# Chunk 1's x^T from 64x32 tiles, with its denominators inverted between two VectorE turns

## The chip, the cores and the metric

The kernel runs on one core of a Trainium2 chip. The metric is device time in microseconds (us) for one execution; three runs of the kernel before gave 258.91, 259.48 and 259.96, median 259.48. The engines are named as in the profile: PE (TensorE, matmuls), PEld (its weight loads), DVE (VectorE), ACT (ScalarE), POOL (GpSimd), SP (SyncE, which here only issues DMAs).

## The reference

An attention with sketched features, and behind it an MLP with an exact GELU:

```python
# q, k, v: (4 batches, 4 heads, 1088 tokens, 32); S1, S2: (8, 32)
def phi(x):
    a = np.einsum('rd,bhsd->bhsr', S1, x)
    b = np.einsum('rd,bhsd->bhsr', S2, x)
    return np.einsum('bhsi,bhsj->bhsij', a, b).reshape(*x.shape[:-1], r * r)
q_p, k_p = (phi(q), phi(k))
kv = np.einsum('bhsf,bhsd->bhfd', k_p, v)
z = np.sum(k_p, axis=2)
num = np.einsum('bhsf,bhfd->bhsd', q_p, kv)
den = np.einsum('bhsf,bhf->bhs', q_p, z)[..., None] + 1e-06
attn_out = (num / den).astype(np.float32)
# x: (4352 tokens, 128 = 4 heads * 32)
h = x @ w_in                                  # w_in: (128, 2048)
g = 0.5 * h * (1.0 + erf(h / np.sqrt(2)))
out = (g @ w_out).astype(np.float32)          # w_out: (2048, 128)
```

w_in, w_out, S1 and S2 arrive as 64-bit floats. The kernel rounds them to 32 bits itself, from the two words of each number.

## The kernel before

The 4352 tokens are eight chunks of 512 (two for each batch) and a last one of 256. x^T of a chunk is a tile of 128 features by 512 tokens. A hidden slice `hidden(n, fi)` (L715) is one matmul of 128 columns of w_in with x^T of chunk n into one of two PSUM banks h_ps, and a GELU on ACT out of it. An output product `project(n, fi)` (L847) adds a slice times its part of w_out to chunk n's o_ps. Chunks 0 and 1 do their first eight slices in this way (`steps`, L964), and everything behind them with seven products in place of eight. The matmul of the first slice stands apart as `first_hidden` (L730): in quarters for chunk 0, in halves for chunk 1.

The order on every engine is the order of the text: each instruction is tied to the one before it on its engine (L1219), so an instruction that waits holds up all behind it on its engine.

Batch 0's keys and values are reduced first into kz[0] (L930), which has 64 features for two pairs of heads on its partitions, and for each head 32 columns of kv and one of z. Then chunk 0 and chunk 1 get their x^T. `expand_products(n)` (L533) multiplies the turned queries with both sketches on PE, ACT copies one factor (`expand_copy`, L548), and DVE multiplies the two into q_pT (`expand_multiply`, L552). In the kernel before, both chunks go on alike: `numerators_by_token` (L648) makes, in tiles of 64x64 with 33 columns, numerators and denominators with tokens on the partitions; `divide` (L663) divides on DVE; `turn_half` (L698) or `turn_half_apart` (L690) transposes the quotient on PE, and ACT or DVE copies it out of PSUM into xT. For chunk 1 this stands in the loop over the steps at t = 3 (L1175 to L1187), with chunk 0's output products among it. Later chunks take another way (`query_outer`, `attend`, L584 to L644) with 64x32 tiles at L633; for batch 0's part of the last chunk they read `kz_first`, which `repeat_first_z` (L498) fills by two ACT copies.

Rounding of a weight piece (class `Rounding`, L243): `low_words` (ACT, L260), two `fields` (DVE, L268 exponent and L273 mantissa), `exponents` (ACT, L279), `mantissas` (DVE, L287, or ACT L284 and POOL L285), `signs` (DVE, L292) and `product` (L297, DVE or POOL). The first two pieces of w_in and of w_out hold 256 columns each. w_in[0]'s product is on POOL; behind it POOL writes one word into the landing place of w_out[0] and of w_out[1] (L180), and SP's queue, which issues in order, has these two transfers waiting for that (L181), and all later weights, keys, values and queries behind them.

In the opening, lines L923 to L961 set the order: chunk 0's numerators and division, chunk 1's expansion, rounding of w_in[1] between the divisions, chunk 0's first slice, chunk 1's q_pT.

Of the kernel before, what the change touches and what calls it, by code (L numbers as in the profile page):

```python
# [8 lines left out]
FP = mybir.dt.float32  # L9
U32 = mybir.dt.uint32  # L10
AX = mybir.AluOpType
# [5 lines left out]
def kernel(  # L17
# [28 lines left out]
    REM = S - MAIN  # L46
    JC = 4
    CW = JC * 128
    G = 128 // 32
    NCH = J // JC  # L50
    C = D + 1
# [25 lines left out]
    def hidden_bank():  # L77
        return hps.tile([128, CW], FP, name="h_ps")

    def out_bank():  # L80
        return ops.tile([128, CW], FP, name="o_ps")

# [144 lines left out]

    kz = [big.tile([128, 128], FP, name=f"kz{b}") for b in range(B)]

    kz_first = big.tile([128, 128], FP, name="kz_first")  # L230

    ones = big.tile([128, D], FP, name="ones")

# [255 lines left out]
    def sketch_of_z(b, ps, at):  # L489
# [5 lines left out]
        dve.tensor_mul(out=S_abc[b][:, :, :, 4:8], in0=c.rearrange("p (i f) -> p i f", i=2)[:, :, None].broadcast_to([128, 2, 2, 4]),  # L495
                       in1=own_r[:, None, :, None].broadcast_to([128, 2, 2, 4]))

    def repeat_first_z():  # L498

        of = kz[0].rearrange("f (r x) -> f r x", r=2)  # L500
        to = kz_first.rearrange("f (c r d) -> f c r d", c=NP, r=2)
        for c in range(NP):
            act.copy(out=to[:F, c], in_=of[c * F:(c + 1) * F, :, 0:D])
        zs = att.tile([128, 2, D], FP, name="z_cols")
        pool.tensor_copy(out=zs, in_=of[:, :, D:C].broadcast_to([128, 2, D]))
        held["zs"] = zs
# [26 lines left out]
    def expand_products(n):  # L533


        W = width[n]
        for i in range(2):
            B_of[n, i] = work_banks()
        for s in range(2):
            for g in range(G):  # L540
                for c in range(NP):
                    rows = slice(g * D, (g + 1) * D)
                    pe.matmul(B_of[n, g // 2][c * F:(c + 1) * F, g % 2, s * W // 2:(s + 1) * W // 2],  # L543
                              lhsT=Srep[rows, s].rearrange("p i j -> p (i j)"),
                              rhs=qT[n][rows, 2 * c:2 * c + 2].rearrange("p r j t -> p r (j t)"), start=True, stop=True)
        qp[n] = att.tile([128, 2, CW], FP, name="q_pT")

    def expand_copy(n, i):  # L548
# [2 lines left out]

    def expand_multiply(n, i):  # L552
        W = width[n]
        a, b = (t.rearrange("f g (r x) -> f g r x", r=2) for t in (A[i][:, :, :W // 2], B_of[n, i][:, :, W // 2:W]))
        dve.tensor_mul(out=qp[n].rearrange("f r (g x) -> f g r x", g=G)[:, 2 * i:2 * i + 2], in0=a, in1=b)

# [64 lines left out]
    def attend_products(n, banks=None):  # L621


        W = width[n]
        m = 1 if n < NMAIN else B // 2
        banks = work_banks() if banks is None else banks
        f = qp[n].rearrange("f r x -> f (r x)")[:, :2 * W].rearrange("f (c i n r t) -> f c i n r t", c=NP, i=m, r=2, t=32)
        N = W // 2 // m
        for i in range(m):
            for s in range(2):  # L630
                rows, b = slice(s * 64, (s + 1) * 64), batch_of(n, s, i)
                for h in range(H):
                    pe.matmul(banks[h * D:(h + 1) * D, s, i * N:(i + 1) * N],  # L633
                              lhsT=(kz[b] if b else kz_first)[rows, h * D:(h + 1) * D],
                              rhs=f[rows, h // 2, i, :, h % 2], start=True, stop=True)
        numerators_in[n] = banks

    def take_x(n):

        W, banks, m = width[n], numerators_in.pop(n), 1 if n < NMAIN else B // 2  # L640
        xT[n] = att.tile([128, CW], FP, name="xT", bufs=3)
        to = xT[n][:, :W]
        to = to.rearrange("p (s x) -> p s x", s=2) if m == 1 else to.rearrange("p (s t i) -> p s i t", s=2, i=m)
        act.copy(out=to, in_=banks[:, :, :W // 2] if m == 1 else banks[:, :, :W // 2].rearrange("p s (i t) -> p s i t", i=m))  # L644

    x_tok = {}

# [92 lines left out]

    blocks, sums, acc = {}, {}, {}
    T = {}
    HW = CW // 2
    NPAIR = NF // 2

    PLACE = {"1": (0, 0, 0), "2": (0, 0, HW), "3": (1, 0, 0), "5": (1, 0, HW),
# [175 lines left out]
    kv_first_rem(kv_bank)  # L922
    w_in = [Rounding(w) for w in w_in_sb[:2]]  # L923
    w_in[0].low_words()
    w_in[0].fields()
    w_in[0].exponents()
    late = []
    query_turn(1, lambda **a: late.append(a))
# [7 lines left out]
    w_out = [Rounding(w, beside=b) for w, b in zip(w_out_sb[:2], w_in)]  # L936
    by_act(**late[0])
    w_in[1].low_words()
    parts = [range(2), range(2, JC)]
    nd = [[hidden_bank(), hidden_bank()], [out_bank(), out_bank()]]  # L940
    for banks, tokens in zip(nd, parts):
        numerators_by_token(0, banks, tokens)
    den = denominators(nd[1])
    expand_products(1)
    divide(0, nd[0], parts[0], by_head_pair=True)
    w_in[1].exponent_fields()
    w_in[1].exponents()
    divide(0, nd[1], parts[1], by_head_pair=True, den=den)
    turn_half(0, 0, hidden_bank(), by_act)
    w_in[1].mantissa_fields()  # L950
    turn_half_apart(0, 1, [out_bank(), out_bank()])
    w_in[1].mantissas()
    w_in[1].signs()
    w_in[1].product()
    for half in range(2):
        first_hidden(0, half)
    for i in range(2):
        expand_copy(1, i)
    for i in range(2):
        expand_multiply(1, i)  # L960
    w_out[0].fields()  # L961


    steps = [(n, fi) for f in range(0, USUAL, 4) for n in range(NCH) for fi in range(f, f + 4)]  # L964
# [199 lines left out]
    for t in range(len(steps) + LAG):  # L1164
        if t < 4:

            hidden(0, t)
            if t == 1:
                w_out[0].low_words()
                w_out[0].exponents()  # L1170
                w_out[0].finish()
                w_out[1].fields()
            if t == 2:
                w_out[1].low_words()
            if t == 3:  # L1175
                banks = work_banks()
                numerators_by_token(1, halves(banks), range(JC))
                w_out[1].mantissas(by_pool=True)
                w_out[1].exponents()
                divide(1, banks, range(JC), by_head_pair=False)  # L1180
                w_out[1].signs()
                w_out[1].product()
                project(0, 0)
                project(0, 1, cols=slice(0, 256))
                turn_half(1, 0, work_bank(), by_act)
                project(0, 1, cols=slice(256, 512))
                turn_half(1, 1, work_bank(), by_dve)  # L1187
            continue
        if t == 4:
            first_hidden(1, 0)  # L1190
            for f, *a in products[t]:
                f(*a)
            first_hidden(1, 1)
        for n in drains[t]:
            drain(n)
        sooner = t == NMAIN * NF
        if sooner:
            for f, *a in products[t]:
                f(*a)
        if t < len(steps):  # L1200
            n, fi = steps[t]
            hidden(n, fi, by_halves=t >= 18 and (n < NMAIN or fi < 5))
        if t < len(steps) and steps[t][0] < NMAIN and steps[t][1] % NB == NB - 1:
            n, b = steps[t][0], steps[t][1] // NB
            if b >= first_block(n):
                token_sums(n, b)
        for f in slots[t]:
            f()
        for n in done[t]:
            store(n)  # L1210
        if t != 4 and not sooner:
            for f, *a in products[t]:
                f(*a)
    for n in done[len(steps) + LAG]:
# [40 lines left out]
```

## Time and profile before

| what | value |
|---|---|
| time, median of three runs | 259.48 us |
| span of the profiled execution, first to last instruction | 258.0 us |
| time of the profiled execution itself | not given apart; the three runs are 258.91 to 259.96 us |
| granted TensorE clock | 1.000 |
| DVE, ACT, POOL busy | 151.0, 115.5, 163.5 us |
| chunk 1's x^T, from its numerators' start to its last turn's end on PE | 19.11 to about 22.4 us |
| chunk 1's first hidden slice, starts of its two halves | 22.45 and 23.81 us |

The profile is that of one execution. A row of a timeline has a start and a length in us from the first instruction, the engine, the line, the operation, the tile written and the tiles read, and the count of instructions that were merged into the row; in brackets stands idle time and what ended it. A 32-bit matmul is recorded as two instructions, a transpose as one. Matmuls are pipelined, so the start of the next row tells more than the length of one.

### The profile page before, as it was taken

The numbers are of one execution on the slowest core, as the hardware profiler recorded it, in microseconds if no ns is written. First come the engines' busy times: TensorE is split into PE (matmuls) and PEld (weight loads), VectorE is DVE, ScalarE is ACT, GpSimd is POOL, SyncE is SP. The second block draws the span as 40 slices with busy tenths as digits, with TensorE's granted clock in tenths as the row PEclk, the third lists the DMA queues.
The fourth block names the chain that finished last, engine by engine and source line by source line (L and its number), as shares of the span: only waits on it lengthen the run. The fifth ranks groups of instructions, "written<-read, shape, count | busy, mean of one in ns | idle before, by whom it ended". The sixth has DMA issues, their size and how long they took to land.

```text
span 258.0 us, 5769 instructions
## 1 busy us (share of the span) xinstructions
PE 253.9 (98%) x2335; PEld 136.1 (53%) x2335; DVE 151.0 (59%) x312; ACT 115.5 (45%) x224; POOL 163.5 (63%) x173
## 2 busy tenths in 40 slices
PE   8999999999999999999999999999999999999995
PEld 7856444345444545544444455455444444445794
DVE  2786888969699997590187986399307000700330
ACT  4685777443626332443335332533444334433442
POOL 3403006799968788487758775787758777877300
PEclk9999999999999999999999999999999999999999
DMA  6469848721000101102000002000200200020020
GB/s 199 144 185 374 188 95 217 213 76 14 3 0 12 31 1 21 23 6 37 3 0 3 0 9 38 0 1 3 41 3 4 39 0 1 7 36 0 3 41 20
DMA packets 29594, 13.48 MB, mean 52 GB/s; under 512 B 21888, under 2 KB 27776, under 8 KB 29568
## 3 DMA queue, kind: packets, MB, share of 16 engines
q1 hardware_dynamic: 29392, 13.05, 20.3%
q8 instruction: 18, 0.29, 0.5%
q10 hardware_dynamic: 176, 0.07, 0.1%
q14 instruction: 8, 0.07, 0.1%
HBM read 10.88 MB, written 2.23 MB: 51 GB/s over the span
## 4 chain that ended last, share of the span: by engine, by line
PE 98%; DVE 1%; issue 0%; ACT 0%; DVEq 0%
PE h_ps L721 45%; PE o_ps L807 33%; PE o_ps L858 5%; PE w_ps L855 3%; PE w_ps L437 1%; PE w_ps L890 1%; PE w_ps L578 1%; PE w_ps L633 1%; PE o_ps L426 1%; PE h_ps L737 1%; PE w_ps L978 1%; PE w_ps L656 0%; PE w_ps L543 0%; DVE x_tok L679 0%; PE h_ps L333 0%; PE w_ps L333 0%
## 5 line engine op out<-in xcount | busy, mean ns | idle before, releaser
L721 PE MATMUL h_ps<-xT,w_in 128*64 128x512 f32 (+3 forms) x514 | 136.9, 576 | 0.0
L728 ACT ACTIVATE block<-h_ps 128x512 f32<-128x512 f32 (+1 forms) x128 | 73.0, 571 | 117.3 <-PE h_ps L721 115.3
L721 PEld LDWEIGHTS h_ps<-xT,w_in 128*64 128x64 f32 (+1 forms) x514 | 41.9, 143 | 30.4 <-issue 11.6
L807 PE MATMUL o_ps<-block,w_out 128*64 128x256 f32 x224 | 57.5, 379 | 0.0
L772 POOL TENSOR_TENSOR bits_low<-block 128x512 f32<-128x512 f32 x28 | 35.9, 1281 | 27.8 <-ACT block L728 27.8
L807 PEld LDWEIGHTS o_ps<-block,w_out 128*64 128x64 f32 x224 | 30.5, 137 | 38.0 <-issue 27.5
L773 POOL TENSOR_TENSOR bits_a<-block 128x512 f32<-128x512 f32 x28 | 35.7, 1277 | 12.0 <-ACT block L728 11.9
L822 DVE COPY sums<-o_ps 64x256 f32<-64x256 f32 x8 | 3.3, 416 | 60.6 <-PE o_ps L807 60.6
L774 POOL TENSOR_TENSOR bits_e<-bits_a,block 128x512 f32<-128x512 f32 x28 | 36.0, 1286 | 2.2
L775 POOL TENSOR_TENSOR bits_m<-block,bits_e 128x512 f32<-128x512 f32 x28 | 35.8, 1279 | 2.2
L807 PE MATMUL o_ps<-bits_low,small 128*64 128x256 f32 x112 | 28.8, 380 | 0.0
L807 PE MATMUL o_ps<-bits_a,small 128*64 128x256 f32 x112 | 28.8, 380 | 0.0
L807 PE MATMUL o_ps<-block,small 128*64 128x256 f32 x112 | 28.8, 379 | 0.0
L807 PE MATMUL o_ps<-bits_m,w_out 128*64 128x256 f32 x112 | 28.8, 380 | 0.0
L807 PEld LDWEIGHTS o_ps<-block,small 128*64 128x64 f32 x112 | 15.2, 137 | 17.9 <-issue 10.8
L807 PE MATMUL o_ps<-bits_e,small 128*64 128x256 f32 x112 | 17.1, 383 | 0.0
L858 PE MATMUL o_ps<-g,w_out 128*128 128x512 f32 (+1 forms) x34 | 16.5, 572 | 0.0
L807 PEld LDWEIGHTS o_ps<-bits_m,w_out 128*64 128x64 f32 x112 | 15.4, 137 | 0.0
L807 PEld LDWEIGHTS o_ps<-bits_a,small 128*64 128x64 f32 x112 | 15.2, 137 | 0.0
L807 PEld LDWEIGHTS o_ps<-bits_low,small 128*64 128x64 f32 x112 | 15.2, 137 | 0.0
L590 DVE STREAM_TRANSPOSE w_ps<-w_ps 128x512 f32<-128x512 f32 (+1 forms) x7 | 4.8, 687 | 17.1 <-ACT xT L644 12.7
L807 PEld LDWEIGHTS o_ps<-bits_e,small 128*64 128x64 f32 x112 | 7.7, 137 | 10.6 <-issue 8.8
(194 smaller groups left out, 305.1 us busy)
## 6 DMA issues: line engine op xcount, KB each, us to landing
block<-in_moe_w_in_dram SPq DMA_DIRECT2D x3, 512.0 KB, 8.4
block<-in_moe_w_out_dram SPq DMA_DIRECT2D x3, 512.0 KB, 12.1
k<-in_k_dram SPq DMA_DIRECT2D x12, 128.0 KB, 3.1
v<-in_v_dram SPq DMA_DIRECT2D x12, 128.0 KB, 3.4
q<-in_q_dram SPq DMA_DIRECT2D x24, 64.0 KB, 2.4
out_dram<-oT SPq DMA_DIRECT2D x21, 64.0 KB, 2.2
k<-in_k_dram SPq DMA_DIRECT2D x2, 256.0 KB, 2.8
q<-in_q_dram SPq DMA_DIRECT2D x2, 256.0 KB, 3.9
```

The source lines that it names most:

```text
L426: pe.matmul(ps[c * F:(c + 1) * F, r * 2 * D:r * 2 * D + C], lhsT=flat(k_p[0, r][:, t, c * 4 + ch * 2 + one]), rhs=v_aug[r][:, c, i, :C], s ...
L590: dve.transpose(out=tok, in_=ps[:, :, :H2])
L721: pe.matmul(ps[rows, :W], lhsT=w[:, rows], rhs=xT[n][:, :W], start=True, stop=True)
L728: act.activation(out=g_of[n, fi][:, :W], in_=ps[:, :W], func=ACT.Gelu)
L772: pool.tensor_sub(out=s[3], in0=a11, in1=a21)
L773: pool.tensor_add(out=s[1], in0=a21, in1=a22)
L774: pool.tensor_sub(out=s[2], in0=s[1], in1=a11)
L775: pool.tensor_sub(out=s[4], in0=a12, in1=s[2])
L807: pe.matmul(acc[n][bank][half * 64:(half + 1) * 64, col:col + HW], lhsT=fixed, rhs=moving, start=opens and e == 0 and name in "4715", stop ...
L822: dve.tensor_copy(out=N[lo, 0, one], in_=a0[lo, one])
L855: pe.matmul(o_of[n][i][:, :128], lhsT=g[:, i * 128:(i + 1) * 128], rhs=w_tile(w_out_sb, fi), start=first, stop=final)
L858: pe.matmul(o_of[n][:, cols], lhsT=w_tile(w_out_sb, fi), rhs=g[:, cols], start=first, stop=final)
```

## The change

Chunk 1 no longer goes by tokens. `spread_first_kv` copies kz[0] by four ACT copies into kz_both, for all four heads and on both halves of the partitions; `spread_first_z` widens the column of z on POOL to 32 equal columns. `expand_products(1)` takes halves of the tokens instead of pairs of heads, so q_pT has a token half on each half of its partitions. `ratio_products` then makes, in 64x32 tiles of 256 columns, first the denominators (each 32 times) and then the numerators, with features on the partitions. `ratio_inverse` turns the denominators in blocks of 32 by 32 on DVE, adds 1e-6 and inverts one of the 32 equal columns; `ratio` turns the inverses back, read 32 times each, and multiplies them with the numerators out of PSUM into xT, in two halves. The numerators by token, four PE transposes, and the two copies out of PSUM of chunk 1 go.

Around it: `fields` and `exponents` of w_in[1] come earlier, ahead of chunk 0's division; w_in[1]'s mantissas and signs come ahead of chunk 0's turn, and its product goes from DVE to POOL; w_out[0]'s fields come ahead of chunk 1's q_pT on DVE; at t = 0 to 3 the rounding steps stand ahead of the step's hidden slice, and w_out[1]'s follow at t = 3; chunk 0's output products 0 to 3 all come ahead of chunk 1's first slice (before, product 2 stood between the slice's halves and product 3 behind chunk 1's second slice). kz_first and its two ACT copies go.

```diff
--- before.py
+++ after.py
@@ -46,6 +46,7 @@
     REM = S - MAIN
     JC = 4
     CW = JC * 128
+    HW = CW // 2
     G = 128 // 32
     NCH = J // JC
     C = D + 1
@@ -227,7 +228,8 @@
 
     kz = [big.tile([128, 128], FP, name=f"kz{b}") for b in range(B)]
 
-    kz_first = big.tile([128, 128], FP, name="kz_first")
+    kz_both = big.tile([128, H, 2 * D], FP, name="kz_both")
+    z_wide = big.tile([128, H, D], FP, name="z_wide")
 
     ones = big.tile([128, D], FP, name="ones")
 
@@ -495,12 +497,19 @@
         dve.tensor_mul(out=S_abc[b][:, :, :, 4:8], in0=c.rearrange("p (i f) -> p i f", i=2)[:, :, None].broadcast_to([128, 2, 2, 4]),
                        in1=own_r[:, None, :, None].broadcast_to([128, 2, 2, 4]))
 
+    def spread_first_kv():
+
+        of = kz[0].rearrange("f (r x) -> f r x", r=2)
+        for s in range(2):
+            for c in range(NP):
+                act.copy(out=kz_both[s * F:(s + 1) * F, 2 * c:2 * c + 2, :C], in_=of[c * F:(c + 1) * F, :, :C])
+
+    def spread_first_z():
+        pool.tensor_copy(out=z_wide, in_=kz_both[:, :, D:C].broadcast_to([128, H, D]))
+
     def repeat_first_z():
 
         of = kz[0].rearrange("f (r x) -> f r x", r=2)
-        to = kz_first.rearrange("f (c r d) -> f c r d", c=NP, r=2)
-        for c in range(NP):
-            act.copy(out=to[:F, c], in_=of[c * F:(c + 1) * F, :, 0:D])
         zs = att.tile([128, 2, D], FP, name="z_cols")
         pool.tensor_copy(out=zs, in_=of[:, :, D:C].broadcast_to([128, 2, D]))
         held["zs"] = zs
@@ -542,7 +551,8 @@
                     rows = slice(g * D, (g + 1) * D)
                     pe.matmul(B_of[n, g // 2][c * F:(c + 1) * F, g % 2, s * W // 2:(s + 1) * W // 2],
                               lhsT=Srep[rows, s].rearrange("p i j -> p (i j)"),
-                              rhs=qT[n][rows, 2 * c:2 * c + 2].rearrange("p r j t -> p r (j t)"), start=True, stop=True)
+                              rhs=(qT[n][rows, :, 2 * c:2 * c + 2] if n else qT[n][rows, 2 * c:2 * c + 2])
+                              .rearrange("p r j t -> p r (j t)"), start=True, stop=True)
         qp[n] = att.tile([128, 2, CW], FP, name="q_pT")
 
     def expand_copy(n, i):
@@ -551,6 +561,10 @@
 
     def expand_multiply(n, i):
         W = width[n]
+        if n:
+            dve.tensor_mul(out=qp[n].rearrange("f r (g x) -> f (r g) x", g=2)[:, 2 * i:2 * i + 2],
+                           in0=A[i][:, :, :W // 2], in1=B_of[n, i][:, :, W // 2:W])
+            return
         a, b = (t.rearrange("f g (r x) -> f g r x", r=2) for t in (A[i][:, :, :W // 2], B_of[n, i][:, :, W // 2:W]))
         dve.tensor_mul(out=qp[n].rearrange("f r (g x) -> f g r x", g=G)[:, 2 * i:2 * i + 2], in0=a, in1=b)
 
@@ -631,7 +645,7 @@
                 rows, b = slice(s * 64, (s + 1) * 64), batch_of(n, s, i)
                 for h in range(H):
                     pe.matmul(banks[h * D:(h + 1) * D, s, i * N:(i + 1) * N],
-                              lhsT=(kz[b] if b else kz_first)[rows, h * D:(h + 1) * D],
+                              lhsT=kz[b][rows, h * D:(h + 1) * D] if b else kz_both[rows, h, :D],
                               rhs=f[rows, h // 2, i, :, h % 2], start=True, stop=True)
         numerators_in[n] = banks
 
@@ -642,6 +656,36 @@
         to = xT[n][:, :W]
         to = to.rearrange("p (s x) -> p s x", s=2) if m == 1 else to.rearrange("p (s t i) -> p s i t", s=2, i=m)
         act.copy(out=to, in_=banks[:, :, :W // 2] if m == 1 else banks[:, :, :W // 2].rearrange("p s (i t) -> p s i t", i=m))
+
+    def ratio_products(n, banks):
+
+        f = qp[n].rearrange("f r (g h t) -> f h (r g) t", g=2, h=H)
+        for at, w in ((HW, lambda rows, h: z_wide[rows, h]), (0, lambda rows, h: kz_both[rows, h, :D])):
+            for s in range(2):
+                rows = slice(s * F, (s + 1) * F)
+                for h in range(H):
+                    pe.matmul(banks[h * D:(h + 1) * D, s, at:at + HW], lhsT=w(rows, h), rhs=f[rows, h], start=True, stop=True)
+
+    def ratio_inverse(banks):
+
+        turned = att.tile([128, 2 * CW], FP, name="q_f", bufs=1)
+        dve.transpose(out=turned[:, :CW].rearrange("p (g s x) -> p s g x", g=G, s=2),
+                      in_=banks[:, :, HW:].rearrange("p s (g x) -> p s g x", g=G))
+        den = att.tile([128, NP, JC * 2], FP, name="den_tok").rearrange("p c k -> p (c k)")
+        dve.tensor_scalar(out=den, in0=turned[:, :CW].rearrange("p (k x) -> p k x", x=D)[:, :, 0], scalar1=1e-6, scalar2=None,
+                          op0=AX.add)
+        dve.reciprocal(out=den, in_=den)
+        return den, turned[:, CW:]
+
+    def ratio(n, banks, den, wide):
+
+        xT[n] = att.tile([128, CW], FP, name="xT", bufs=3)
+        for i in range(2):
+            cols = slice(i * HW, (i + 1) * HW)
+            dve.transpose(out=wide[:, cols], in_=den[:, i * 8:(i + 1) * 8, None].broadcast_to([128, 8, D]))
+            by = lambda t: t.rearrange("p (g s x) -> p s g x", g=2, s=2)
+            dve.tensor_mul(out=by(xT[n][:, cols]), in0=banks[:, :, i * 128:(i + 1) * 128].rearrange("p s (g x) -> p s g x", g=2),
+                           in1=by(wide[:, cols]))
 
     x_tok = {}
 
@@ -740,7 +784,6 @@
 
     blocks, sums, acc = {}, {}, {}
     T = {}
-    HW = CW // 2
     NPAIR = NF // 2
 
     PLACE = {"1": (0, 0, 0), "2": (0, 0, HW), "3": (1, 0, 0), "5": (1, 0, HW),
@@ -922,7 +965,8 @@
     kv_first_rem(kv_bank)
     w_in = [Rounding(w) for w in w_in_sb[:2]]
     w_in[0].low_words()
-    w_in[0].fields()
+    for w in w_in:
+        w.fields()
     w_in[0].exponents()
     late = []
     query_turn(1, lambda **a: late.append(a))
@@ -936,29 +980,29 @@
     w_out = [Rounding(w, beside=b) for w, b in zip(w_out_sb[:2], w_in)]
     by_act(**late[0])
     w_in[1].low_words()
+    w_in[1].exponents()
     parts = [range(2), range(2, JC)]
     nd = [[hidden_bank(), hidden_bank()], [out_bank(), out_bank()]]
     for banks, tokens in zip(nd, parts):
         numerators_by_token(0, banks, tokens)
     den = denominators(nd[1])
+    spread_first_kv()
+    spread_first_z()
     expand_products(1)
     divide(0, nd[0], parts[0], by_head_pair=True)
-    w_in[1].exponent_fields()
-    w_in[1].exponents()
     divide(0, nd[1], parts[1], by_head_pair=True, den=den)
-    turn_half(0, 0, hidden_bank(), by_act)
-    w_in[1].mantissa_fields()
-    turn_half_apart(0, 1, [out_bank(), out_bank()])
     w_in[1].mantissas()
     w_in[1].signs()
-    w_in[1].product()
+    w_in[1].product(pool)
+    turn_half(0, 0, hidden_bank(), by_act)
+    turn_half_apart(0, 1, [out_bank(), out_bank()])
     for half in range(2):
         first_hidden(0, half)
     for i in range(2):
         expand_copy(1, i)
+    w_out[0].fields()
     for i in range(2):
         expand_multiply(1, i)
-    w_out[0].fields()
 
 
     steps = [(n, fi) for f in range(0, USUAL, 4) for n in range(NCH) for fi in range(f, f + 4)]
@@ -1164,32 +1208,31 @@
     for t in range(len(steps) + LAG):
         if t < 4:
 
-            hidden(0, t)
             if t == 1:
                 w_out[0].low_words()
                 w_out[0].exponents()
                 w_out[0].finish()
+            if t == 3:
+                w_out[1].low_words()
                 w_out[1].fields()
-            if t == 2:
-                w_out[1].low_words()
-            if t == 3:
-                banks = work_banks()
-                numerators_by_token(1, halves(banks), range(JC))
                 w_out[1].mantissas(by_pool=True)
                 w_out[1].exponents()
-                divide(1, banks, range(JC), by_head_pair=False)
+            hidden(0, t)
+            if t == 2:
+                banks = work_banks()
+                ratio_products(1, banks)
+            if t == 3:
+                inverse = ratio_inverse(banks)
                 w_out[1].signs()
                 w_out[1].product()
+                ratio(1, banks, *inverse)
                 project(0, 0)
-                project(0, 1, cols=slice(0, 256))
-                turn_half(1, 0, work_bank(), by_act)
-                project(0, 1, cols=slice(256, 512))
-                turn_half(1, 1, work_bank(), by_dve)
+                project(0, 1)
             continue
         if t == 4:
+            for f, *a in products[t] + products[t + 1]:
+                f(*a)
             first_hidden(1, 0)
-            for f, *a in products[t]:
-                f(*a)
             first_hidden(1, 1)
         for n in drains[t]:
             drain(n)
@@ -1208,7 +1251,7 @@
             f()
         for n in done[t]:
             store(n)
-        if t != 4 and not sooner:
+        if t not in (4, 5) and not sooner:
             for f, *a in products[t]:
                 f(*a)
     for n in done[len(steps) + LAG]:
```

## The prediction

> **What bounds the kernel now.** I read the totals by engine first, then the chain of work that ended last, then the timeline of each engine over the opening, which is all the change touches.
>
> ```profile
> PE 253.9 (98%) x2335; PEld 136.1 (53%) x2335; DVE 151.0 (59%) x312; ACT 115.5 (45%) x224; POOL 163.5 (63%) x173
> ...
> PE 98%; DVE 1%; issue 0%; ACT 0%; DVEq 0%
> ```
>
> TensorE (PE) is busy for 98% of the span and carries 98% of the chain. So an edit on another engine is worth only the TensorE time it frees or stalls. The timeline of PE over chunk 1's opening (columns: start, length, engine, line, operation, tiles, count; a matmul counts twice, a transpose once):
>
> ```profile
> 15.38 1.13 PE L737 MATMUL h_ps<-xT,w_in 128*128 128x128 f32 x8
> 16.35 2.84 PE L721 MATMUL h_ps<-xT,w_in 128*128 128x512 f32 x6
> 19.11 1.14 PE L656 MATMUL w_ps<-kz,q_pT 64*64 64x33 f32 x64
> 20.18 1.56 PE L858 MATMUL o_ps<-g,w_out 128*128 128x512 f32 x4
> 21.57 0.38 PE L702 MATMUL w_ps<-ident,x_tok 128*128 128x128 f32 x2
> ...
> 23.81 0.59 PE L737 MATMUL h_ps<-xT,w_in 128*128 128x256 f32 x2
> 24.24 1.02 PE L721 MATMUL h_ps<-xT,w_in 128*128 128x512 f32 x2
> ```
>
> I go by starts, since lengths include the pipeline's tail. A 512-column matmul costs 0.86 (24.24 to 25.10). From 15.38 to 24.24, 8.86 us, PE does eight such units (chunk 0's first hidden slice in quarters, hidden slices 1 to 3, output products 0 to 2, chunk 1's first hidden slice in halves): 8 x 0.86 = 6.88. The other **1.98 us** is chunk 1's x^T: the products by token 1.07 (19.11 to 20.18), 0.18 ahead of them, four transposes of 0.11 (21.57 to 21.79 for two), and 0.30 of small gaps.
>
> **The change part by part.**
>
> *PE, chunk 1.* Removed: those products and transposes. Added: 16 matmuls in 64x32 tiles with 256 columns. The same form runs at L633: eight from 68.99 to 69.42, 0.43, so sixteen 0.86. Entering and leaving: at L978 the tiles start 0.09 after the wide matmul is due to end (43.13 + 0.86 = 43.99, start 44.08), and the next full matmul comes 0.16 beyond 0.43 (44.67). Sum 0.86 + 0.25 = 1.11; between 0.86 and 1.3. Of the 0.30 of gaps, 0.11 (16.24 to 16.35) stays. Saving 1.98 - 0.11 - 1.11 = **0.76**.
>
> *Ahead of 15.38.* DVE loses a field conversion (13.90, about 0.2) between two divisions, but the denominators from ScalarE come 0.15 later, since `exponents` of w_in[1] now precedes them (L687 at 13.46 becomes about 13.61). The second division starts near 14.25, not 14.40, and PE's 0.21 wait at 15.04 goes. What is late next is ScalarE's copy of xT (14.86 to 15.23), so the first hidden slice starts at 15.30: a gain of 0.08. The four new copies to kz_both stand ahead of that copy: two of nearly this size (L503) take 0.49, so four 0.98, from 13.83 to 14.81. They just fit; without the 0.05 of room each further 0.1 costs 0.1.
>
> *The new wait on a transfer.* w_out[0]'s fields now stand ahead of the two q_pT multiplies on DVE, and PE's ratio products wait for these. Before:
>
> ```profile
> 16.82 1.28 DVE L555 TENSOR_TENSOR q_pT<-A_sb,w_ps 128x512 f32<-128x512 f32 x2
> 18.01 0.29 DVE L268 TENSOR_SCALAR bits_e<-small 128x256 uint32<-128x256 uint32 x1
> ```
>
> The transfer and its gate:
>
> ```profile
> 13.21 0.12 POOL L180 MEMSET small<- 1x1 uint32 x2
> 13.33 1.81 SPq L181 DMA_DIRECT2D small<-in_moe_w_out_dram  x2
> ```
>
> The DMA view gives 3.0 from issue to landing for the first of the two: 16.33. The earliest reader before is ScalarE at 17.90, which waits for no DMA, so 17.90 bounds it from above. The gate follows w_in[0]'s product, which follows its `signs` on DVE; w_in[1]'s two fields (0.20 apart at 11.10 and 11.30; its data, issued at 6.61 with 3.8 to land, is there by 10.4) now stand ahead of those: 0.2 later for the gate and every weight transfer behind it on SP's queue. None but this one is near its reader (DVE reads the first block of w_in at 22.99, and in the new order near 23.4; the keys issued at 19.10 took 11.5 and are read at 40.88). So w_out[0] lands at 16.53, the fields take 0.4, q_pT ends near 18.25, and the ratio products start at 18.30. PE has ended hidden slice 2 at 17.99 and could start at 18.09: a wait of **0.21**. I take the landing from the DMA view, as it is a measured row.
>
> *w_in[1]'s product on POOL.* 0.73 (L297) from about 15.55 gives 16.3; its reader, hidden slice 2, comes at 17.1. Hidden. w_in[1]'s `mantissas` and `signs` ahead of DVE's xT copy put that at 15.46 (15.48 before): nothing.
>
> *Behind the ratio products.* They end at 19.16, hidden slice 3 starts at 19.32, the four output products run from 20.18 to 23.62, and chunk 1's first hidden slice follows. On DVE behind q_pT: rounding of w_out[0] to about 19.3, two fields, the turn of the denominators (0.69 as L590) from 19.69, the addition and reciprocal to 20.9, w_out[1]'s signs and product to 21.8, a turn of 256 columns (0.69 for 512 and 1.245 for 1024, so about 0.41), a multiply of 0.43: first half of xT at 22.6, second at 23.4. PE wants them at 23.62 and 24.05: covered by 1.0 and 0.65. w_out[1] is wanted at 21.90 and ready at 21.87: no room. The reading of den by a stride of nought in a turn is in no row; between 0.3 and 0.7 each, I take 0.41, and both ends stay inside the 1.0. If the cover were gone, the chain from 18.73 (first products done) to 22.6 would cost all its 3.9.
>
> *Sum.* 0.76 + 0.08 - 0.21 = **0.63** earlier at equal work. By the clock: chunk 1's first slice ends at 24.48 with four output products done, against 24.24 + 0.86 = 25.10 before: 0.62. After this PE runs back to back (24.24 to 43.13 is 22 x 0.86), DVE waits there for ScalarE and ScalarE for PE, so all move together. Nearest to a stall is w_in[2]: before, its product ended at 28.2 for a use at 29.39; now near 28.5 for 28.78. The two late kz_first copies on ScalarE (0.49) free no PE time.
>
> The profiled span is 258.0; its own time beyond that is not given. The median 259.48 lies 1.4 above the span. 0.6 off the span is 257.4, and off the median **258.9**.
>
> **A rule weighed.** VectorE and POOL slow each other where both read SBUF:
>
> ```profile
> 43.49 0.90 POOL L761 TENSOR_TENSOR small<-w_out,small 128x128 f32<-128x128 f32 x1
> 43.99 0.94 DVE L292 SCALAR_TENSOR_TENSOR bits_e<-block,bits_r 128x512 uint32<-128x512 uint32 x1
> ```
>
> Alone they take 0.45 and 0.69, so DVE loses 0.25. In the change z_wide's copy on POOL (near 14.85, some 0.35) falls on w_in[1]'s mantissas and signs. If `signs` loses 0.25 to 0.35, DVE's xT copy ends near 16.1, not 15.75, while its reader, the fourth quarter, is due at 15.94: PE loses about 0.25. The Trainium skill (SBUF — State Buffer, Who interferes with whom) says that a VectorE instruction with two SBUF inputs contends with a GpSimd instruction that reads SBUF, and that the second to issue blocks fully; by that rule the trace agrees in kind, though both rows are slowed rather than one blocked, and the time would be 259.1.
>
> **The rivals.**
>
> 1. *DVE or ScalarE eats the gain*: the collision above, the four copies a little longer, or w_out[1]'s product 0.2 to 0.3 late. For it: room of 0.05 and nought in two places. Against: each is paid once. Gain 0.1 to 0.35: **259.2**.
> 2. *More than counted*: the landing is early or its wait hides in the change of tiles, the tiles leave free of cost. 0.63 + 0.21 + 0.25 = 1.1: **258.4**. For it: the 0.18 ahead of L656 may be a part of the same wait.
> 3. *Slower*: w_out[0] lands near 17.9 instead of 16.33, and DVE stands at its fields with q_pT behind, and PE behind that. At 18.10 with the later gate the ratio products start at 19.87, 1.57 later: 1.57 - 0.63 = 0.94 slower, **260.4**. It decides from a landing 0.63 later than I take. For it: two weight transfers share the DMA engines there, and the second took 4.4. Against: the measured 3.0.
> 4. *The turns are not hidden*: DVE's chain ends over 1.0 late, by broadcast turns at several times 0.41. One us over the cover: 259.9.
>
> **How the numbers follow.** Forecast 0.52, rival 1 0.16, rival 2 0.14, rival 3 0.12, rival 4 0.06. The median's own spread is 258.91 to 259.96, so each case blurs by some 0.4. The forecast's own range is 258.5 to 259.3. The range for 8 in 10 takes in rivals 1 and 2 and most of 3 and stops at 258.0 and 260.2. About 0.5% (1.3 us) is what a measurement of this kernel can tell from no change: faster by more needs rival 2 and a blur (0.12); slower by more needs rival 3 or 4 beyond its price (0.07); the rest, 0.81, lies within.
>
> **What would show it.** Right: ratio products near 18.3 for about 0.86; the second L737 group of chunk 1 ending near 24.5 with four output products ahead of it; equal later work 0.6 earlier. Wrong: DVE idle at w_out[0]'s fields with a DMA as releaser beyond 16.6 (rival 3); PE waiting for xT at the first hidden slice of chunk 1 (rival 4); ScalarE's xT copy starting after 14.9 (rival 1); any later PE gap at w_in[2].

## The result, and the profile after

The kernel after takes 259.75 us (median of 22 runs, 259.10 to 260.86) against 259.49 us (22 runs of the kernel before, 258.76 to 259.96): ratio 1.0018, interval 1.0009 to 1.0026. The forecast was 258.9, so the time moved 0.26 the other way, and the interval leaves out 1. It is inside the stated range (258.0 to 260.2) and within the 0.5% of "the same", but not where the mechanism put it. The profiled execution took 260.15 us with a span of 258.4.

The totals by engine and the chain of work that ended last, kernel after:

```profile
PE 253.7 (98%) x2297; PEld 134.2 (52%) x2297; DVE 151.4 (59%) x311; ACT 115.4 (45%) x225; POOL 165.1 (64%) x175
...
PE 90%; DMA 3%; DVE 2%; SPq 2%; issue 1%; POOL 0%; ACT 0%; DVEq 0%
```

PE's work shrank a little (253.9 to 253.7, 38 instructions fewer). But the chain, 98% PE before, now leaves PE for DMA, SP's queue and DVE: transfers have come onto the path. The timeline of PE shows where. Columns as in the prediction; L667 are the ratio products, L765 hidden slices, L781 first slices, L901 output products:

```profile
15.20 1.13 PE L781 MATMUL h_ps<-xT,w_in 128*128 128x128 f32 x8
16.16 2.04 PE L765 MATMUL h_ps<-xT,w_in 128*128 128x512 f32 x4
18.53 0.67 PE L667 MATMUL w_ps<-q_pT,z_wide 64*32 64x256 f32 x16 [0.33 <-DVE q_pT L565]
18.99 0.64 PE L667 MATMUL w_ps<-q_pT,kz_both 64*32 64x256 f32 x16
19.56 1.12 PE L765 MATMUL h_ps<-xT,w_in 128*128 128x512 f32 x2
20.52 1.88 PE L901 MATMUL o_ps<-g,w_out 128*128 128x512 f32 x4
22.61 1.96 PE L901 MATMUL o_ps<-g,w_out 128*128 128x512 f32 x4 [0.21 <-DVE w_out L299]
24.41 1.03 PE L781 MATMUL h_ps<-xT,w_in 128*128 128x256 f32 x4
25.27 2.04 PE L765 MATMUL h_ps<-xT,w_in 128*128 128x512 f32 x4
27.14 1.02 PE L901 MATMUL o_ps<-g,w_out 128*128 128x512 f32 x2
```

The state that the forecast put at 24.48 (chunk 1's first slice and four output products done) is reached at 25.27, against 25.10 before. Counted from chunk 0's first slice, where after is 0.18 ahead (15.20, before 15.38), that is 10.07, against 9.72 before and the forecast's 9.18 (15.30 to 24.48). Two waits stand in it. One is ahead of the ratio products, the other ahead of the third output product: the row at 22.61 could have begun at 22.24, two matmuls of 0.86 behind 20.52 and so 0.37 earlier (the trace's own 0.21 counts from the modelled end of the pipeline). DVE over the same stretch, kernel after:

```profile
11.89 0.29 DVE L270 TENSOR_SCALAR bits_e<-small 128x256 uint32<-128x256 uint32 x1 [0.48 <-DMA small<-in_moe_w_in_dram]
...
16.79 0.29 DVE L270 TENSOR_SCALAR bits_e<-small 128x256 uint32<-128x256 uint32 x1 [1.17 <-DMA small<-in_moe_w_out_dram]
...
17.20 1.28 DVE L565 TENSOR_TENSOR q_pT<-A_sb,w_ps 128x512 f32<-128x512 f32 x2
...
20.67 0.68 DVE L675 TENSOR_SCALAR den_tok<-q_f 128x16 f32<-128x16 f32 x1
...
22.02 0.44 DVE L299 TENSOR_TENSOR w_out<-bits_m,bits_e 128x256 f32<-128x256 f32 x1
22.39 0.43 DVE L685 STREAM_TRANSPOSE q_f<-den_tok 128x256 f32<-128x256 f32 x1
```

DVE stands twice for a transfer, at w_in[1]'s field (0.48) and at w_out[0]'s (1.17). Then the addition of 1e-6 to 16 denominators per partition takes 0.68, where before the like addition (L673, out of PSUM) took 0.17; w_out[1]'s product is behind it. And POOL, kernel after:

```profile
13.81 0.12 POOL L181 MEMSET small<- 1x1 uint32 x2
...
20.60 0.72 POOL L287 TENSOR_TENSOR bits_m<-bits_high,bits_low 128x256 f32<-128x256 f32 x1 [4.37 <-ACT bits_high L286]
```

The gate of w_out's transfers opens at 13.81 (before 13.21), and while POOL makes w_out[1]'s mantissas from two SBUF tiles (20.60 to 21.32), DVE's little addition does not end: 21.35.

Pieces of the chain that ended last (start, length, what), kernel after, from w_in[1]'s transfer to the late output product:

```profile
6.61 5.26 DMA small<-in_moe_w_in_dram
...
11.89 0.04 DVE bits_e L270
...
13.14 0.73 POOL w_in L299
13.87 0.06 POOL small L181 x2
13.93 2.83 DMA small<-in_moe_w_out_dram
...
20.67 0.70 DVE den_tok L675
...
22.02 0.46 DVE w_out L299
22.48 0.14 issue
22.61 1.96 PE o_ps L901 x4
```

Both transfers and the addition lie on one chain, most of it in DVE's queue; PE joins it only at 22.61.

**A way to add it up.** In all 14 traces of this study, the span is three stretches: up to chunk 0's numerators on PE, from there to the start of chunk 1's fourth GELU ("the stretch" below), and the rest, which is 229.3 each time (229.29 to 229.34). So what a version wins or loses is in the second, and what it happens to start with is in the first. The table also has how long w_in[1]'s transfer took from its issue at 6.6 to its landing:

| kernel, execution | w_in[1]'s transfer | numerators start | stretch | span |
|---|---|---|---|---|
| before | 3.8 | 12.28 | 16.46 | 258.0 |
| before, again | 5.5 | 12.03 | 16.46 | 257.8 |
| after | 5.3 | 12.09 | 16.97 | 258.4 |
| after, second | 5.3 | 11.54 | 17.48 | 258.3 |
| after, third | 3.7 | 12.25 | 16.14 | 257.7 |

The kernel before has the same stretch in both executions, though the transfer took 1.7 longer in one of them. The kernel after has three: the shortest where the transfer came early, the longest where the numerators started furthest ahead of a late one.

### The profile page after: what moved, and what is told of

The parts are those of the page before. It is cut to its first block, busy times and chain, and to the rows that moved or that the text cites. A ratio compares the mean times of both kernels' runs of the same rounds, so it can differ in the third digit from the quotient of the medians.

```text
span 258.4 us, 5694 instructions
## 1 busy us (share of the span) xinstructions
PE 253.7 (98%) x2297; PEld 134.2 (52%) x2297; DVE 151.4 (59%) x311; ACT 115.4 (45%) x225; POOL 165.1 (64%) x175
## 4 chain that ended last, share of the span: by engine, by line
PE 90%; DMA 3%; DVE 2%; SPq 2%; issue 1%; POOL 0%; ACT 0%; DVEq 0%
PE h_ps L765 44%; PE o_ps L850 33%; PE o_ps L901 5%; PE w_ps L898 3%; DMA small<-in_moe_w_in_dram 2%; PE w_ps L439 1%; PE w_ps L592 1%; PE w_ps L647 1%; DMA small<-in_moe_w_out_dram 1%; SPq L133 1%; SPq L101 1%; PE w_ps L1022 1%; DVE bits_e L294 0%; SPq L119 0%; DVE w_out L299 0%
## 5 line engine op out<-in xcount | busy, mean ns | idle before, releaser
L765 PE MATMUL h_ps<-xT,w_in 128*64 128x512 f32 (+3 forms) x514 | 137.2, 576 | 0.0
L765 PEld LDWEIGHTS h_ps<-xT,w_in 128*64 128x64 f32 (+1 forms) x514 | 41.7, 142 | 30.7 <-issue 11.9
L901 PE MATMUL o_ps<-g,w_out 128*128 128x512 f32 x32 | 16.1, 596 | 0.2 <-DVE w_out L299 0.2
```

Of the source, the lines that this page charges most:

```text
L765: pe.matmul(ps[rows, :W], lhsT=w[:, rows], rhs=xT[n][:, :W], start=True, stop=True)
L901: pe.matmul(o_of[n][:, cols], lhsT=w_tile(w_out_sb, fi), rhs=g[:, cols], start=first, stop=final)
```

## The experiments

Theories. *Landings*: two field conversions now stand in DVE's queue ahead of work that PE waits for, and what they read lands at a time that differs between executions. *Port*: the addition reads and writes SBUF and stands still while POOL reads two SBUF tiles. Rivals: the ratio's own path is longer than the old one (tiles or turns), the new order costs it all, or the addition is slow by itself. Times are medians of 11 or 12 runs beside the kernel before on the same chip (259.53; 259.44 for e8 and e9).

**The new ratio in the old order.** w_in[1] is converted between the divisions as before, on DVE throughout, and w_out[0]'s fields stand behind q_pT:

```diff
-    for w in w_in:
-        w.fields()
+    w_in[0].fields()
...
+    w_in[1].exponent_fields()
+    w_in[1].exponents()
     divide(0, nd[1], parts[1], by_head_pair=True, den=den)
+    w_in[1].mantissa_fields()
...
-    w_in[1].product(pool)
+    w_in[1].product()
```

> The new x^T of chunk 1 (with its order of hidden slices and output products) with the old order of the conversions: w_in[1]'s fields and exponents between chunk 0's divisions, its mantissas, signs and product on DVE behind the turn, w_out[0]'s fields behind q_pT. By theories A and D DVE's chain is the bound and the order was made to shorten it: the ratio products start on PE's time (6.0 us after chunk 0's numerators), the addition of 1e-6 still stands behind POOL's w_out[1] mantissas and takes 0.5 to 0.7, and PE waits some 0.6 to 0.8 for w_out[1]'s product; 0.2 to 0.5 us slower than the kernel before, so 259.7 to 260.0. Rival (the new order is the whole loss, the tiles save 0.6): 0.4 to 0.7 faster than the kernel before.

259.94 us, ratio 1.0015 (1.0005 to 1.0026), stretch 17.58. So the new order alone is not what loses. Rows of DVE and PE:

```profile
21.05 0.63 DVE L675 TENSOR_SCALAR den_tok<-q_f 128x16 f32<-128x16 f32 x1
```

```profile
22.93 1.96 PE L901 MATMUL o_ps<-g,w_out 128*128 128x512 f32 x4 [0.50 <-DVE w_out L299]
```

The addition is long again, and w_out[1] is later still: products 0 and 1 began at 20.55, so 22.27 was due and 0.66 is lost. This trace also has an idle 0.43 on PE among the numerators, ahead of anything the change touches, whose releaser it does not show; I leave that part of the 17.58 open.

**The new order with the old x^T.** The kernel before, with both field pairs and the w_in[1] conversion where the change has them:

```diff
-    w_in[0].fields()
+    for w in w_in:
+        w.fields()
...
+    w_out[0].fields()
     for i in range(2):
         expand_multiply(1, i)
-    w_out[0].fields()
```

> The new order of the conversions (w_in[1]'s fields and exponents early, its mantissas and signs ahead of chunk 0's turn, its product on POOL, w_out[0]'s fields ahead of q_pT) with the old x^T of chunk 1 by tokens. By theories A and D nothing is lost: the numerators by token stand behind hidden slice 3 on PE, a whole slice later than the ratio products, so a q_pT that is late by 0.4 is hidden, and the addition of 1e-6 reads PSUM; within 0.15 us of the kernel before. Rival (the new order is the loss): 0.3 to 0.6 slower.

259.56, ratio 1.0006 (0.9996 to 1.0016): no difference in the time. The trace missed the expectation: stretch 16.80, 0.34 over before. Its DVE row:

```profile
11.51 0.29 DVE L268 TENSOR_SCALAR bits_e<-small 128x256 uint32<-128x256 uint32 x1 [0.83 <-DMA small<-in_moe_w_in_dram]
```

The opening was quick (numerators at 11.36), the data were not there, and the divisions stood behind the field. So the order can lose in the trace, as it did in this execution.

**The w_in[1] fields behind w_in[0]'s signs**, so that the gate does not wait for them:

```diff
-    for w in w_in:
-        w.fields()
+    w_in[0].fields()
...
     w_in[0].signs()
+    w_in[1].fields()
     w_in[0].product(pool)
```

> Edit: w_in[1]'s two field conversions go behind w_in[0]'s signs on DVE. Theory A (the new order puts a transfer's landing into DVE's queue, and DVE's chain from w_out[0]'s fields to w_out[1]'s product is what PE waits for): DVE no longer stands 0.48 us at w_in[1]'s fields, the gate's memset on POOL comes near 13.2 instead of 13.81, w_out[0] lands 0.6 earlier, the ratio products start near 18.0 instead of 18.53, w_out[1]'s product is 0.5 to 0.6 earlier; 0.5 to 0.7 us less than the changed kernel (259.75), so 259.05 to 259.25. Rival B (the 64x32 tiles and their turns themselves are what costs): 0.2 or less. Rival C (w_in[1] lands no later than 10.4 and the wait was a stray of one run): no change.

259.57, ratio 1.0009 (0.9997 to 1.0020), stretch 16.70. The landing wait on w_in[1] is gone, but two conversions now lie beside POOL's products and take 0.82 and 0.51 in place of 0.29, and the addition takes 0.69. What one mechanism gave, the other took: 0.18 less than the change's 259.75, where 0.5 to 0.7 was expected.

**The w_out[0] fields behind q_pT**:

```diff
-    w_out[0].fields()
     for i in range(2):
         expand_multiply(1, i)
+    w_out[0].fields()
```

> Edit: w_out[0]'s fields go behind chunk 1's two q_pT multiplies on DVE, as in the kernel before. Theory A: DVE's idle time of 1.17 us ahead of those fields goes, q_pT ends near 17.25, the ratio products start at PE's own time near 18.0, and DVE's chain behind is 0.7 to 0.8 earlier; 0.6 to 0.9 us less than the changed kernel. Rival B: 0.2 or less, since the same work stands on both engines.

259.33, ratio 1.0001 (0.9990 to 1.0013), stretch 16.16. Rows of PE:

```profile
17.88 0.66 PE L667 MATMUL w_ps<-q_pT,z_wide 64*32 64x256 f32 x16
...
19.87 3.64 PE L901 MATMUL o_ps<-g,w_out 128*128 128x512 f32 x8
23.35 1.03 PE L781 MATMUL h_ps<-xT,w_in 128*128 128x256 f32 x4
```

The ratio products come 6.04 behind the numerators' start (11.84), in place of 6.44, with no wait, and the four products stand back to back, in one row. Here w_in[1] was in time, too, so the trace does not show what this edit alone gives: the unedited third execution has 16.14. The time is 0.42 below the change's, where 0.6 to 0.9 was expected.

**The turned denominators in PSUM**, so that the addition reads no SBUF:

```diff
-        turned = att.tile([128, 2 * CW], FP, name="q_f", bufs=1)
+        turned = work_banks()[:, 0]
+        wide = att.tile([128, 2 * CW], FP, name="q_f", bufs=1)[:, CW:]
```

> Edit: the first turn writes into a free PSUM bank, so the addition of 1e-6 reads PSUM and not SBUF; nothing else moves. Theory D (the addition, 0.68 us in the changed kernel for 16 elements a partition, stood behind POOL's w_out[1] mantissas, which read SBUF from 20.60 to 21.32, at a port they share): the addition takes 0.15 to 0.25, w_out[1]'s product comes 0.45 earlier, PE's wait at chunk 0's output product 2 (22.25 to 22.61) goes, 0.3 to 0.4 us less than the changed kernel. Rival E (an access of 128-byte steps or a drain behind the turn is what is slow): it stays at 0.6 or more and the time does not move.

259.44, ratio 1.0008 (0.9995 to 1.0021), stretch 16.11. The time is 0.31 below the change's, as expected (0.3 to 0.4). DVE, then POOL:

```profile
20.26 0.17 DVE L676 TENSOR_SCALAR den_tok<-w_ps 128x16 f32<-128x16 f32 x1
```

```profile
20.08 0.72 POOL L287 TENSOR_TENSOR bits_m<-bits_high,bits_low 128x256 f32<-128x256 f32 x1 [3.84 <-ACT bits_high L286]
```

Both run at the same time, and the addition takes 0.17. So the slow part is the SBUF side of the addition; the step of its reads and its place behind the turn, the rival, are the same here. In the six traces with the turn in SBUF it ends 0.03 behind POOL's instruction; in the five with it in PSUM it takes 0.17 each time. What it is worth to PE: from the ratio products to chunk 1's second slice pass 6.74 in the first two executions of the kernel after (18.53 to 25.27), 6.56 with e1, and 6.28 here (18.30 to 24.58). Where w_in[1] lands early, the addition costs PE little even in SBUF: 6.31 in the third execution, so e3's stretch of 16.11 is hardly below that one's 16.14. The Trainium skill (SBUF — State Buffer, Who interferes with whom) says that VectorE and GpSimd share a port pair that one holds for a whole instruction, and (VectorE: DVE Perf Modes, Mode 2×_2P — use both read ports for one tensor) that tensor_scalar can take both read ports, and only from SBUF. By that rule, the traces agree, 0.68 against 0.17.

**All three edits together** (e1, e2, e3):

> All three edits together. Theories A and D: PE waits neither for q_pT nor for w_out[1], ratio products near 18.0, 0.8 to 1.0 us less than the changed kernel, 0.4 to 0.6 less than the kernel before (the 0.6 of the forecast). Rival B: no more than 0.4 less than the changed kernel, so still no faster than the kernel before.

259.09, ratio 0.9985 (0.9971 to 1.0000), stretch 16.23. The best median of the study, though its interval touches 1. Against the changed kernel the gain is clear of noise: the interval lies wholly below the change's 1.0009 to 1.0026, as those of the next two versions do. It is 0.66 less than the change, where 0.8 to 1.0 was expected.

**Two of them, and the products no longer together** (e2, e3, and output product 3 behind chunk 1's second slice):

```diff
-            for f, *a in products[t] + products[t + 1]:
+            for f, *a in products[t]:
...
-        if t not in (4, 5) and not sooner:
+        if t != 4 and not sooner:
```

> The changed kernel with w_out[0]'s fields behind q_pT, the first turn in PSUM, and chunk 0's output product 3 again behind chunk 1's second hidden slice, so that two hidden slices of chunk 1 do not stand back to back behind one GELU. In the two runs with the turn in PSUM PE lost some 0.15 between chunk 1's second slice and the output product behind the third (1.87 us where two units are 1.72). Theory: that goes; from chunk 0's numerators to chunk 1's fourth GELU 15.95 us, against 16.46 before and 16.97 in the changed kernel; 0.5 less than the kernel before, so about 259.0. Rival (the turns are not ready for the earlier first slice): PE waits up to 0.4 for xT, and it is no faster than the changed kernel with the turn in PSUM.

259.28, ratio 0.9993 (0.9982 to 1.0003), stretch 15.99, the shortest of all and near the 15.95 expected; the time of 259.0 expected with it did not come. Rows of PE:

```profile
23.73 1.02 PE L766 MATMUL h_ps<-xT,w_in 128*128 128x512 f32 x2
24.59 1.02 PE L902 MATMUL o_ps<-g,w_out 128*128 128x512 f32 x2
25.44 1.02 PE L766 MATMUL h_ps<-xT,w_in 128*128 128x512 f32 x2
26.30 1.02 PE L902 MATMUL o_ps<-g,w_out 128*128 128x512 f32 x2
```

Starts 0.86 apart. In the kernel after, chunk 1's second and third slices stand together at 25.27, and the next product comes 1.87 later, not 1.72 (2 x 0.86): the third slice waits for the first one's GELU to free its bank. That is 0.15.

**All four edits** (e1 too):

> The best so far with w_in[1]'s fields behind w_in[0]'s signs as well. Theory A: chunk 0's division no longer depends on w_in[1]'s landing; but those fields now fall on POOL's product of w_in[0], which reads SBUF, and one of them takes 0.8 instead of 0.29 as in the two runs with this edit, so the division is 0.1 to 0.3 late every time. From chunk 0's numerators to chunk 1's fourth GELU 16.05 to 16.3 us; 0.3 to 0.6 less than the kernel before. Rival (the landing hardly ever counts): as the best so far or 0.2 slower.

259.31, ratio 0.9995 (0.9986 to 1.0004), stretch 16.29. w_in[1]'s transfer took 3.8 here, so the e1 part had no wait to take away, and the stretch is 0.30 longer than e6's. The time is 0.13 below the kernel before, where 0.3 to 0.6 was expected. DVE's field, then POOL's product:

```profile
12.49 0.84 DVE L275 TENSOR_SCALAR bits_a<-small 128x256 uint32<-128x256 uint32 x1
```

```profile
12.46 0.73 POOL L299 TENSOR_TENSOR w_in<-bits_m,bits_e 128x256 f32<-128x256 f32 x1 [2.47 <-DVE bits_e L294]
```

The field starts 0.03 behind POOL, and ends only after it: the same pattern on another pair of instructions.

**No conversion ahead of its data** (e6, with the w_in[1] conversion where the kernel before has it; two of the kz_both copies and z_wide go behind chunk 0's first GELU to make room on ACT):

```diff
-    spread_first_kv()
-    spread_first_z()
+    spread_first_kv((0,))
...
             if t == 1:
+                spread_first_kv((1,))
+                spread_first_z()
                 w_out[0].low_words()
```

> The best so far with w_in[1]'s fields where the kernel before has them (one behind the first division, one behind the second), its exponents on ACT behind two of the four kz_both copies, and the other two copies and z_wide behind chunk 0's first GELU. No conversion of w_in[1] stands ahead of w_in[0]'s signs, and no field falls on a product of POOL. Theories A and D: from chunk 0's numerators to chunk 1's fourth GELU 15.95 to 16.05 us in any execution, however early the numerators start; 0.4 to 0.7 less than the kernel before. Rival: the two late copies make the ratio products or hidden slice 2 wait, 16.2 or more.

259.38, ratio 1.0002 (0.9992 to 1.0012), stretch 16.56. The rival of this run was right: ACT's late copies push back w_out[0]'s low words, and DVE stands for them:

```profile
17.98 0.43 DVE L289 SCALAR_TENSOR_TENSOR bits_m<-bits_a,bits_low 128x256 f32<-128x256 uint32 x1 [0.45 <-ACT bits_low L262]
```

Chunk 1's x^T is late with that: its first slice takes from 22.88 to 24.02, 0.28 over its 0.86 (0.22 over in e8, without late copies). That is half of the 0.57 by which this stretch is longer than e6's; I do not place the rest. The landing itself cost nothing: the transfer took 5.3, and DVE has no wait for it.

**The change, again and a third time; the kernel before, again.** No edit; these ask whether the stretch is the kernel's or the execution's.

> The changed kernel once more, unedited, for the spread of its landings. Theory D: the addition of 1e-6 ends within 0.05 us of POOL's w_out[1] mantissas again. Theory A: where w_in[1] lands by 11.5 us, DVE does not stop at its fields and the ratio products start near 6.05 us after chunk 0's numerators instead of 6.44; where it lands later, the start moves by as much. Time as measured, 259.6 to 259.9.

> The changed kernel a third time, unedited. Theory A: the later w_in[1]'s fields start after the numerators, the longer the stretch to chunk 1's fourth GELU: 16.5 us with no wait there, 16.97 as in the first profile, 17.48 as in the second. Theory D: the addition of 1e-6 ends within 0.05 us of POOL's w_out[1] mantissas.

> The kernel before once more, unedited. Theory A: its own stretch from chunk 0's numerators to chunk 1's fourth GELU is 16.46 us also where the numerators start earlier than 11.54 us after the first load, since w_in[1]'s first field stands behind the division. Rival (the stretch varies as much without the change): it differs by 0.3 or more.

The second execution (259.82 against 259.53, ratio 1.0011, 1.0001 to 1.0020) started early and waited more. DVE, then PE:

```profile
11.93 0.29 DVE L270 TENSOR_SCALAR bits_e<-small 128x256 uint32<-128x256 uint32 x1 [1.07 <-DMA small<-in_moe_w_in_dram]
...
20.62 0.69 DVE L675 TENSOR_SCALAR den_tok<-q_f 128x16 f32<-128x16 f32 x1
```

```profile
14.14 0.41 PE L746 MATMUL h_ps<-ident,x_tok 128*128 128x128 f32 x2 [0.42 <-DVE den_tok L718]
```

Its numerators started 0.55 before those of the first trace, and its w_in[1] field at 11.93 against 11.89: the transfer, not the engines, set it, and PE now waits at chunk 0's first turn as well. The third (one run, 259.47) had no wait for w_in[1]:

```profile
18.29 0.66 PE L667 MATMUL w_ps<-q_pT,z_wide 64*32 64x256 f32 x16
...
20.27 3.62 PE L901 MATMUL o_ps<-g,w_out 128*128 128x512 f32 x8
23.73 1.03 PE L781 MATMUL h_ps<-xT,w_in 128*128 128x256 f32 x4
24.60 2.04 PE L765 MATMUL h_ps<-xT,w_in 128*128 128x512 f32 x4
```

That is nearly the forecast's timeline: 18.30 for the ratio products, 23.62 for the first slice, 24.48 for its end. With the data early, POOL's mantissas and the addition overlap by less (0.44 for the addition), and w_out[1] is just in time. The kernel before, again (one run, 259.59), has the stretch of 16.46 to the hundredth. Its numerators did not start as early as the expectation asked (12.03, not before 11.54), but w_in[1]'s transfer took 5.5, the longest of all traces, and cost nothing: its field stands at 13.66, behind the first division.

## Why the prediction was wrong, step by step

- **The tiles and turns were nearly right.** Ratio products to the next hidden slice: 1.03 (18.53 to 19.56), forecast 1.02. Going into the tiles costs the forecast's 0.09 (e2, where q_pT is ready: the last half of hidden slice 2 starts on PE at 17.36, is due to end at 17.79, and the products start at 17.88). What the sum left out is ahead of that: the two hidden slices at 15.91 take 1.88, not 1.72. In the eleven traces with w_in[1]'s product on POOL they take 1.88 to 1.94, and the second starts 0.14 to 0.15 behind the end of the GELU of chunk 0's first slice, whose bank it needs; with that product on DVE (before, twice, and e4) they take 1.81. The traces do not show why these differ. The 0.16 hides in the forecast's 0.21 of waiting: 3.00 from chunk 0's first slice to the ratio products by the sum, 2.94 in the third execution. The four kz_both copies took 1.02 (forecast 0.98), the turn of the denominators 0.71 (forecast 0.69, a mean at L590 that mixes one turn of 256 columns with six of 512), the broadcast turn 0.43 (forecast 0.41) and w_in[1]'s product hid on POOL. Rival 4 did not happen: x^T was ready before PE asked in the kernel after.
- **"w_out[1] is wanted at 21.90 and ready at 21.87: no room" failed.** The sum gives the addition and the reciprocal 0.52 together (20.38 to 20.9), as the rows at 20.32 and 20.53 of before would allow (0.17 and 0.25), and that addition reads PSUM. The new one reads SBUF beside POOL and took 0.68 and 0.69 in two of three traces. The product was ready 3.93 behind the ratio products' start, not 3.57, and PE lost 0.37 where the sum had nought. I weighed the port rule, but at z_wide: there signs took 0.51 for 0.42 and PE lost nothing. The rule was right and its place wrong. e3 shows the cause of the 0.68. Rival 1 named this product as a place of no room ("0.2 to 0.3 late"), for no stated cause, and as a smaller gain, not a loss.
- **The landing term was mis-sized: 0.40 and 0.91, not 0.21.** Ratio products came 6.44 and 6.95 behind the numerators in the first two executions, and 6.04 in the third and in e2, e3 and e6. w_out[0]'s transfer was right: 2.98 from the gate's start to its reader, forecast 3.12. The gate was not: 13.81 in place of 13.41, because "its data, issued at 6.61 with 3.8 to land, is there by 10.4" came from one execution. That transfer took 5.3 in the first two executions of the kernel after and 3.7 in the third; over the 14 traces it is 3.7 to 5.5. Rival 3 had the kind of mechanism (a transfer with DVE's queue behind it) but the wrong transfer. That its price of 0.94 is near the second execution's 1.02 (17.48 - 16.46) is chance, since that holds the addition too.
- **Small terms left out: 0.33.** The start gain of 0.08 did not come: numerators to first slice is 3.11 after, 3.10 before. From hidden slice 3 to the first output product is 0.96, not 0.86. And 0.15 went to two hidden slices behind one GELU, which the prediction passed over with "PE runs back to back". So 0.63 - 0.33, and 0.06 (3.00 - 2.94) to the good, leaves 0.36 at best; the third execution shows 0.32 (16.46 - 16.14).
- **Behind the opening the prediction held.** From chunk 1's fourth GELU to the end is 229.30 before and 229.31 after; w_in[2] made no gap.

Together: from the third execution's 16.14, the first pays 0.40 for landings and 0.43 between ratio products and chunk 1's second slice, of which 0.37 stands ahead of the third output product, for w_out[1]: 16.97. The median loses 0.26, between the best of these (-0.32) and the worst (+1.02), less what an early start gives back. The profiles show both mechanisms; e2 takes away the wait for w_out[0] and e3 the long addition, while the wait for w_in[1] was away by itself in both. In the times e1, e2 and e3 differ from the kernel before by less than their intervals; e123, e6 and e8, which join e2 and e3, have intervals wholly below the changed kernel's. Three things stay open: why w_in[1]'s landing differs between executions of one program, e4's 0.43, and half of what e9 lost.

## What to carry to other kernels

Price an added instruction by the memory its operands lie in and by what the neighbour engine does in that moment, not by its size: 16 elements cost 0.17 or 0.68. Put the conversion of loaded data into an in-order queue only behind the work that must not wait for it, since one profile shows one landing. And split the span at a point behind which all versions run alike; 0.3 us that medians blur is then plain in the traces.

## What the runs showed of the hardware

- The addition of 16 elements per partition stood until POOL's instruction was over: it took from 0.44 to 0.69 by how far POOL was, and ended 0.03 behind it. A field of 0.29 took 0.82 to 0.85 in the three runs that put it beside POOL's product of w_in[0]. Not every pair does so: z_wide's copy beside signs cost only 0.09.
- The same program's numerators started between 11.54 and 12.25 in three executions, and its w_in[1] field waited 0, 0.48 or 1.07 for the transfer, which took 3.7 or 5.3.
- Between full matmuls, going into 64x32 tiles cost 0.09 (e2, 17.79 to 17.88; after, 43.45 + 0.86 to 44.40) and leaving them 0.14 (after, 18.99 + 0.43 to 19.56).
- A 256-column turn that reads 8 values per partition by a stride of nought took 0.43, no more than plain ones of 256 columns in the kernel before (0.40 at L528, 0.47 at L590).
